# Taking the squares of the next batch out of the vector queue over four products

## The chip, the cores and the metric

The kernel runs on one core of one Trainium2 chip. The metric is the time of one execution on the device in microseconds (us). A profile records one execution; its span is some 1.8 us shorter than the time given for that execution, and the positions below (at 188.6 us, say) count from the span's start. PE is TensorE, DVE is VectorE, ACT is ScalarE; PEld is the loading of weights into PE. L735 and the like are lines of the kernel; behind the change, the lines from 637 on are higher by four (L735 became L739, L642 became L646).

## The reference

```python
scores = scale * q @ k.T                       # batch 8, 12 heads, 448 rows, 64 wide
attn   = np.maximum(scores, 0) ** 2 / 448
x      = (attn @ v)  -> (3584, 768)
h      = x @ w_in                              # 768 -> 2048
g      = np.maximum(h, 0) ** 2                 # relu, then the square
out    = g @ w_out                             # 2048 -> 768, float32
```

## The kernel before

All instructions are laid out by the program that writes the kernel: each engine then runs its own list, in order. Batches are handled in pairs. For each pair the kernel first computes h for its two batches and then `g @ w_out`, one *group* of two blocks of 128 rows after the other. A group is seven products of eight matmuls (a Strassen-Winograd scheme: seven products in place of eight, at the price of operand sums on DVE). Between them stand steps of the attention of later batches ("visits": scores on PE, relu on ACT, squares of `at` on DVE).

Relus and squares of g for the later batches of a pair are not put into DVE's list at once. They go into a queue, `due_g`, and are taken out where a rough model of time has room, or all at once when a group needs them:

```python
def put(d):                                     # take the first of a queue
    ready, cost, fn, _ = d.popleft()
    at_ve[0] = max(at_ve[0], at_pe[0], ready) + cost
    fn()
def fill(until):                                # as many as the model has room for
    for d in (due, due_g):                      # due: squares of the attention
        while d and max(at_ve[0], at_pe[0], d[0][0]) + d[0][1] <= until:
            put(d)
def flush_g(b):                                 # all that batch b and those before it have left
    while due_g and due_g[0][3] <= b:
        put(due_g)
...
def ahead(i, k=n):                              # operand sum s_i of group k
    if k < len(groups) and i not in sets[k]:
        flush_g(max(2 * p + (tb > 2) for p, tb in groups[k] if (p, tb) not in saved))
        sums(i, groups[k], sets[k])
...
def end6(): copy("u2"); ahead(3)                # after the third product: s3, read by the fifth
def end5(): ahead(4)                            # after the fourth: s4, read by the seventh
def end7(): copy("u3"); plus(1, c1, "u3")       # after the fifth: ACT copies u, DVE adds it (osb)
def end4(): ...; ahead(1, n + 1); ahead(2, n + 1)
...
def run():                                      # matmul f of product k of group n
    ...
    if f == 0 and k == 0:
        ahead(1); ahead(2)
    nc.tensor.matmul(acc[0][:, 0:HALF], lhsT=left()[:, f], rhs=right[:, f], ...)
    if f == KH - 1:
        end()
        fill(at_pe[0] + AFTER[k])
```

The first product of the next group is placed ahead of the sixth of the present one. It reads g directly, row block f with matmul f.

## Time and profile before

| | |
|---|---|
| time, median of the first 3 runs | 375.21 us (374.9 to 375.5) |
| span of the profiled run | 373.3 us |
| PE busy | 361.8 us, 97% |
| DVE busy | 279.7 us, 75% |
| ACT busy | 247.6 us, 66% |
| waits of PE, all | 6.0 us |

PE is the bound. The other engines matter where PE waits for them, and a wait on PE moves all that follows.

### The profile page before, as it was taken

The numbers are of one execution on the slowest core, as the hardware profiler recorded it, in microseconds if no ns is written. First come the engines' busy times: TensorE is split into PE (matmuls) and PEld (weight loads), VectorE is DVE, ScalarE is ACT, GpSimd is POOL, SyncE is SP. The second block draws the span as 40 slices with busy tenths as digits, with TensorE's granted clock in tenths as the row PEclk, the third lists the DMA queues.
The fourth block names the chain that finished last, engine by engine and source line by source line (L and its number), as shares of the span: only waits on it lengthen the run. The fifth ranks groups of instructions, "written<-read, shape, count | busy, mean of one in ns | idle before, by whom it ended". The sixth has DMA issues, their size and how long they took to land.

```text
span 373.3 us, 8793 instructions
## 1 busy us (share of the span) xinstructions
PE 361.8 (97%) x3600; PEld 230.7 (62%) x3600; DVE 279.7 (75%) x518; ACT 247.6 (66%) x370; POOL 107.1 (29%) x128
## 2 busy tenths in 40 slices
PE   7999999999999999999989999999999999999994
PEld 3554444445555777875545578887555689975663
DVE  1886677996766787798866758989966688995442
ACT  2997895796676999876546588887665885531220
POOL 8545431837442344431044044050000000000001
PEclk9999999999999999999999999999999999999999
DMA  7999999999999999997799699792233300002333
GB/s 115 199 204 205 205 204 158 122 149 132 215 171 137 171 103 100 114 107 62 136 143 108 151 175 83 92 100 52 49 87 87 84 2 2 2 0 68 95 91 87
DMA packets 121159, 42.64 MB, mean 114 GB/s; under 512 B 100832, under 2 KB 117760, under 8 KB 121120
## 3 DMA queue, kind: packets, MB, share of 16 engines
q0 software_dynamic: 82912, 23.01, 61.9%
q1 hardware_dynamic: 38048, 18.98, 25.7%
q8 instruction: 28, 0.46, 0.5%
q10 hardware_dynamic: 160, 0.10, 0.1%
q14 instruction: 11, 0.09, 0.1%
HBM read 45.61 MB, written 11.01 MB: 152 GB/s over the span
## 4 chain that ended last, share of the span: by engine, by line
PE 86%; DVE 5%; ACT 5%; issue 2%; DMA 1%; POOLq 0%; POOL 0%; DVEq 0%; ACTq 0%
PE mm L735 32%; PE mm L552 26%; PE slot L254 10%; PE mm L422 9%; PE slot L319 7%; ACT at L258 4%; DVE at L371 2%; DMA q<-in_q_dram 1%; PE slot L225 1%; DVE s L608 1%; DVE xt L285 1%; DVE osb L642 1%; DVE g L500 1%; PE mm L225 0%; ACT u L637 0%
## 5 line engine op out<-in xcount | busy, mean ns | idle before, releaser
L258 ACT ACTIVATE at<-slot 128x896 f16<-128x896 f32 x168 | 146.0, 920 | 28.0 <-PE slot L254 28.0
L371 DVE TENSOR_TENSOR at<-at 128x896 f16<-128x896 f16 x168 | 99.1, 618 | 11.4 <-ACT at L258 11.3
L108 POOL DMA_DIRECT2D qs<-in_q_dram x36 | 35.3, 983 | 116.9 <-DMA qT<-qs 109.8
L735 PEld LDWEIGHTS <-s 128*128 128x128 f16 x440 | 41.4, 98 | 33.2 <-issue 3.6
L254 PE MATMUL slot<-qT,kT 64*64 64x448 f16 x756 | 57.4, 360 | 1.6 <-ACT at L258 0.9
L552 PEld LDWEIGHTS <-w 128*128 128x128 f16 x576 | 54.3, 98 | 5.2 <-issue 4.3
L552 PE MATMUL mm<-xt,w 128*128 128x224 f16 x432 | 49.0, 259 | 0.0
L735 PEld LDWEIGHTS <-g 128*128 128x128 f16 x336 | 31.6, 98 | 26.2 <-issue 4.7
L552 PEld LDWEIGHTS <-ws 128*128 128x128 f16 x432 | 40.3, 98 | 4.7 <-issue 4.7
L735 PE MATMUL mm<-b,g 128*128 128x384 f16 x224 | 40.9, 326 | 1.9 <-DVE g L500 1.9
L735 PE MATMUL mm<-b,s 128*128 128x384 f16 x216 | 39.6, 327 | 0.3 <-DVE s L608 0.2
L422 PE MATMUL mm<-xt,w 128*128 128x448 f16 x192 | 39.8, 354 | 0.0
L642 DVE SCALAR_TENSOR_TENSOR osb<-mm,u 128x384 f32<-128x384 f32 (+1 forms) x30 | 16.2, 542 | 30.9 <-ACT u L637 19.8
L735 PE MATMUL mm<-t,s 128*128 128x384 f16 x224 | 39.3, 326 | 0.0
L108 POOL DMA_DIRECT2D ks<-in_k_dram x36 | 35.1, 976 | 10.2 <-DMA b<-in_moe_w_out_dram 5.8
L254 PEld LDWEIGHTS <-kT 64*64 64x64 f16 x756 | 19.6, 104 | 28.9 <-issue 23.9
L575 POOL DMA_DIRECT2D out_dram<-osb x2 | 1.1, 564 | 120.0 <-DVE osb L642 120.0
L637 ACT ACTIVATE u<-mm 128x384 f32<-128x384 f32 x28 | 13.8, 491 | 31.6 <-PE mm L735 30.4
L552 PE MATMUL mm<-x,ws 128*128 128x224 f16 x288 | 34.1, 259 | 0.0
L319 PE MATMUL slot<-at,vt 64*64 64x448 f16 x588 | 31.9, 350 | 0.2 <-DVE at L371 0.2
L500 DVE TENSOR_TENSOR g<-g 128x896 f16<-128x896 f16 x48 | 29.8, 620 | 1.1
L493 DVE TENSOR_TENSOR g<-mm,m 128x448 f16<-128x448 f32 x36 | 22.1, 620 | 10.4 <-PE mm L552 7.1
(69 smaller groups left out, 394.5 us busy)
## 6 DMA issues: line engine op xcount, KB each, us to landing
out_dram<-osb SPq DMA_DIRECT2D x52, 192.0 KB, 3.2
vt<-in_v_dram POOLq DMA_DIRECT2D x24, 224.0 KB, 6.1
qs<-in_q_dram POOLq DMA_DIRECT2D x36, 112.0 KB, 4.5
ks<-in_k_dram POOLq DMA_DIRECT2D x36, 112.0 KB, 5.2
w<-in_moe_w_in_dram POOLq DMA_DIRECT2D x8, 384.0 KB, 11.9
b<-in_moe_w_out_dram POOLq DMA_DIRECT2D x4, 768.0 KB, 17.1
q<-in_q_dram POOLq DMA_DIRECT2D x6, 224.0 KB, 7.7
k<-in_k_dram POOLq DMA_DIRECT2D x6, 224.0 KB, 8.1
```

Source lines behind the costliest of these rows:

```text
L108: nc.gpsimd.dma_start(out=t[:, :, hh, :], in_=heads(src, n)[:, hh].rearrange("p (j d) -> p j d", d=D))
L254: nc.tensor.matmul(ps[c, hh, 0:S], lhsT=kT[r, j, c], rhs=qT[r, :, c], start=True, stop=True)
L258: nc.scalar.activation(out=at, in_=ps[:, :, 0:S], func=AF.Relu, scale=SK)
L319: nc.tensor.matmul(ps[64 * hh:64 * hh + 64, hp, 0:S], lhsT=vt[r, hh, j * D:(j + 1) * D], rhs=at[r, hh, :], start=(j == 0), stop=(j == J - 1))
L371: lambda: nc.vector.tensor_mul(at, at, at), 0))
L422: nc.tensor.matmul(cell[0][:, 0:S], lhsT=w1[f // 4][:, m, (f % 4) * P:(f % 4 + 1) * P], rhs=xts[b][:, m, :], start=(m == 0), stop=(m == NM ...
L493: nc.vector.tensor_add(gs(s, hi, right), acc(s, y), keep[s, nm])
L500: due_g.append((t, 0.54, lambda: nc.vector.tensor_mul(g, g, g), b))
L552: nc.tensor.matmul(XY[s][y][:, r * Q:(r + 1) * Q], lhsT=left(k, i0 + 2 * s + r, m), rhs=right(k, m), start=(fresh and r == 0 and m == 0), ...
L637: nc.scalar.activation(out=t, in_=X[0][:, 0:HALF], func=AF.Copy, scale=CO)
L642: nc.vector.scalar_tensor_tensor(out=osb[row][:, c], in0=acc[0][:, 0:cc.stop - cc.start], scalar=CO, in1=keep[nm][:, cc], op0=ALU.mult, op ...
L735: nc.tensor.matmul(acc[0][:, 0:HALF], lhsT=left()[:, f], rhs=right[:, f], start=(fresh and f == 0), stop=(f == KH - 1), skip_group_check=n ...
```

## The change

The intent: put the squares that the next group will need into DVE's list evenly over the first four products of the present group, instead of leaving what the model found no room for to the moment at which the next group starts.

```diff
+            def needs(k):
+                return max(2 * p + (tb > 2) for p, tb in groups[k]
+                           if (p, tb) not in saved)
+
             def ahead(i, k=n):
                 if k < len(groups) and i not in sets[k]:
-                    flush_g(max(2 * p + (tb > 2) for p, tb in groups[k]
-                                if (p, tb) not in saved))
+                    flush_g(needs(k))
                     sums(i, groups[k], sets[k])
...
                     if f == KH - 1:
                         end()
+                        if k < 4 and n + 1 < len(groups):
+                            some = sum(d[3] <= needs(n + 1) for d in due_g)
+                            for _ in range(-(-some // (4 - k))):
+                                put(due_g)
                         fill(at_pe[0] + AFTER[k])
```

## The prediction

> **What bounds the kernel now.** I read the page first. TensorE (PE) is busy 361.8 of 373.3 us, VectorE (DVE) 279.7, ScalarE (ACT) 247.6, so the kernel ends when its matmul stream ends, and another engine costs time only where a matmul waits for it. So the second view is the list of waits for PE alone: what it waited for, us in total, times, longest. It has eight rows and 6.0 us in all; the three largest are
>
> ```profile
> PE mm L735 <- DVE g L500: 1.9, 1, 1.9
> PE slot L203 <- DVE zeros L157: 1.2, 1, 1.2
> PE slot L254 <- ACT at L258: 0.9, 4, 0.3
> ```
>
> The second row is the start-up. The first is a single wait of a product of the last matrix multiplication (L735) for a square of the batch (L500, the multiplication of g with itself), the very instruction that the change moves. Third view: the chain of waits, in order of time, around that place (start, length, what).
>
> ```profile
> 182.85 1.35 PE slot L319 x28
> 184.23 0.92 ACT xt L325
> 185.15 0.68 ACT at L258
> 185.83 0.04 issue
> 185.87 0.50 ACT u L637
> 186.39 0.56 DVE osb L642
> 186.95 1.07 DVE at L371 x2
> 188.02 0.55 DVE g L500
> 188.56 0.05 issue
> 188.61 0.50 PE mm L735 x2
> ```
>
> In nearly all the rest of this stretch the chain is PE from one line to the next. Here it leaves PE: two ACT evictions, an ACT copy u, the DVE sum that needs u, two attention squares, and only then the last square of g, which PE needs. Fourth view, the timeline of the same place, for the size of the loss:
>
> ```profile
> 185.61 1.14 PE L735 MATMUL mm<-b,g 128*128 128x384 f16 x6
> ...
> 188.61 0.11 PEld L735 LDWEIGHTS <-g 128*128 128x128 f16 x2 [2.25 <-DVE g L500]
> 188.61 0.50 PE L735 MATMUL mm<-b,g 128*128 128x384 f16 x2 [1.86 <-DVE g L500]
> ```
>
> Eight matmuls of a product take 1.30 us (one starts at 172.06, the next at 173.36), or 0.1625 each. Six started at 185.61, so the seventh was due at 185.61 + 6 x 0.1625 = 186.58. It started at 188.61: **2.03 us lost** (the view says 1.86, because it counts modelled ends; its row for weight loads says 2.25). The seventh and eighth row blocks of g are what the last square of the second batch of the pair writes.
>
> **What the Trainium skill says.** "TensorE: Matmul & The Clock Gate", section "Architectural detail: the array is 16× 32×32, not 1× 128×128", says that the queues of ACT and DVE are strictly first in, first out, and that only weight loads can be pulled ahead on PE. The trace agrees: the last square had its input at 185.33 (end of the relu L498 before it), yet stood behind the sum, which DVE idled 1.06 us for, until u came. "VectorE: DVE Perf Modes", section "The perf-mode tier table", gives a multiplication of two 16-bit tensors two elements per cycle and an operation on one tensor four. The trace agrees in order: 896 elements take 0.62 us squared and 0.38 us through the relu. The relus and squares keep these costs; only their places change. "TensorE: Matmul & The Clock Gate", section "Part 1: The HAM clock gate", says the clock is throttled after an idle window of about 3.4 us. A 2 us wait is shorter, and the table by stage has the granted clock at 1.00 from 164 to 290 us, so I expect no clock effect in either direction.
>
> **The change part by part.** The kernel builds its instruction order when it is written out: squares and relus of g sit in a queue, are taken out where a rough model of time has room, and all the rest at the last moment by the next product group. The change takes an even share of those that the next group needs out of the queue at the end of each of the first four products. Nothing is added or removed. Set beside each other, the two programs have the same order on PE, ACT, POOL and SP; on DVE 436 rows stay 436, and the order differs in two places only: one stretch of the second pair of batches (around 178 to 188 us) and one of the third (261 to 269 us). The first pair has no such squares in the queue, and in the last pair the order is the same.
>
> *Second pair, gain.* The new order from 177.55 is: square, relu (448), square, one attention square, two sums osb, relu, square, relu (896), three attention squares, the operand sum s3, square, relu, s4, the last square, and only now the sum that waits for u. Start-to-start times of DVE, from the timeline: square or attention square 0.53 to 0.54, relu 0.30 of either size with a square behind it where it shows, osb 0.47, s 0.60. Chained from 177.55 the two osb start at 179.45 and, held by PE as before, 180.0; the three attention squares at 181.6, 182.1, 182.7; s3 at 183.2 and ends at 183.9; the last square starts at 185.25 and ends at 185.9. The first product that reads s3 starts at 184.30, the attention product reads the last of its squares at about 183.6 (finished 182.8), and the seventh matmul is due at 186.58. So all three are met, by 0.35, 0.8 and 0.7 us: the whole 2.03 us go. Behind it the sums and attention squares come as they did, and DVE idles 2.6 us between 190 and 195, so nothing is handed on.
>
> *Third pair, loss.* Here PE waits for nothing from 252 to 285 us in the profile of before. The squares are pulled ahead of s3, which is on the path soon. The rows that matter, before:
>
> ```profile
> 260.99 0.27 DVE L498 TENSOR_SCALAR g<-g 128x448 f16<-128x448 f16 x1
> 261.50 0.56 DVE L642 SCALAR_TENSOR_TENSOR osb<-mm,m 128x384 f32<-128x384 f32 x1 [0.24 <-issue]
> 261.97 1.15 DVE L371 TENSOR_TENSOR at<-at 128x896 f16<-128x896 f16 x2
> 263.04 0.68 DVE L608 TENSOR_TENSOR s<-g 128x1024 f16<-128x1024 f16 x1
> ...
> 264.45 1.46 PE L735 MATMUL mm<-b,s 128*128 128x384 f16 x8
> ```
>
> s3 ends at 263.72, and the product that takes it as weights starts at 264.45: 0.73 us to spare. New order after the relu at 260.99: square, osb, relu, square, relu (896), two attention squares, s3. Chained: square 261.29, osb 261.83, relu 262.30, square 262.60, relu 263.14, attention squares 263.44 to 264.51, s3 264.51 to 265.19. At 336 us the profile has a product released by such an s3: it starts 0.06 after its end. So the product starts at 265.25 instead of 264.45: **0.80 us of new wait**. (Four instructions moved ahead, 0.54 + 0.30 + 0.54 + 0.30 = 1.68 us, less the 0.24 idle that they fill, is 1.44; 0.73 of it was slack; with 0.06 for the release that is 0.77, the same within the rounding of the pitches.) The next group's first product there did not wait in the kernel before, so the third pair gains nothing back. s4, wanted at 270.9, is ready near 267.7.
>
> Sum: 375.21 - 2.03 + 0.80 = **374.0 us**, 0.33% faster.
>
> **The rivals.** (1) *Gain alone*: s3 of the third pair is in time after all, because DVE gets through faster than my chain. For it: 0.7 us is only a little over one DVE instruction. Against: the order is fixed, each step is a measured pitch, and four instructions stand ahead. It would give 375.21 - 2.03 = 373.2. (2) *The wait moves*: in the second pair s3 or the attention squares come too late, and PE waits there for them. For it: they are delayed 1.7 us and s3 keeps only 0.35 us. If the margin were missed by half a microsecond, the time would be 374.5. If the entire gain were lost, 376.0. (3) *The gain is absorbed later*: PE comes 2 us earlier and meets a transfer or a backlog of DVE or ACT. For it: POOL waits for transposes and DVE is at 75%. Against: PE has no wait of over 0.4 us after 189 us, q and k are fetched two units ahead by the program, and the attention's steps shift with PE. It would give about 375. (4) *The end is not PE*: against it, the stream of matmuls runs unbroken from 339 us to the end, so a shift of it reaches the end whole.
>
> **Range and chances.** The three runs of before spread 0.6 us. Between gain alone (373.2) and a gain half lost (374.9) lies what I hold likely: 373.2 to 374.9, centre 374.0. Two per cent is 7.5 us; no wait in reach has that size, and the largest loss I can construct is below 2 us. Faster by 2%: 0.01, same 0.98, slower 0.01.
>
> **What would show each step.** Right: the list of PE waits no longer has the row for g L500 of 1.9 us; the chain around 186 us stays on PE; a new PE wait of about 0.8 us for DVE s L608 appears near 263 us (264.45 less the 2.03 gained), one row with one wait; PE's end 1.2 us earlier. Wrong: a wait for g L500 that remains at about 185 us, a wait for s L608 near 184 us, no wait near 263 us (then 373.2), or new waits for at L258 or a transposed tile after 190 us.

## The result, and the profile after

The change takes 373.82 us (median of 4 runs, 373.78 to 373.89), beside 375.36 us for the kernel before (median of 4 runs, three of them the runs above, and one of 376.62). The ratio is 0.9954, 95% interval 0.993 to 0.9978: 0.46% less time, which counts as the same at 2%. Ratios here are those of runs of the same rounds; they lie within 0.001 of the ratio of the mean times, so they are not the ratio of the medians.

First view after: the waits of PE, its two largest rows of nine.

```profile
PE slot L203 <- DVE zeros L157: 1.2, 1, 1.2
PE mm L739 <- DVE s L608: 0.9, 2, 0.7
```

The row for g L500, 1.9 us, is gone, and the row for s L608 has grown from 0.2 us in one wait to 0.9 in two. Second view: the chain of waits in the stretch that left PE for seven steps before (start, length, what).

```profile
182.73 1.32 PE slot L319 x28
184.05 0.19 PE slot L254 x4
184.24 2.71 PE mm L739 x16
186.94 0.50 PE slot L254 x8
187.45 4.01 PE mm L739 x24
```

It stays on PE. The eight matmuls of the next group's first product now run without a break, and DVE's timeline shows why: the last square is done at 185.73, ahead of the sum that waits for ACT's u.

```profile
185.12 0.61 DVE L500 TENSOR_TENSOR g<-g 128x896 f16<-128x896 f16 x1
186.26 0.56 DVE L646 SCALAR_TENSOR_TENSOR osb<-mm,u 128x384 f32<-128x384 f32 x1 [0.53 <-ACT u L641]
```

Third view: the timeline in the third pair.

```profile
261.35 1.15 DVE L371 TENSOR_TENSOR at<-at 128x896 f16<-128x896 f16 x2
262.42 0.68 DVE L608 TENSOR_TENSOR s<-g 128x1024 f16<-128x1024 f16 x1
...
260.98 1.47 PE L739 MATMUL mm<-t,s 128*128 128x384 f16 x8
263.16 1.47 PE L739 MATMUL mm<-b,s 128*128 128x384 f16 x8 [0.71 <-DVE s L608]
```

A product takes 1.31 us from start to start, so the second was due at 262.29 and started at 263.16: 0.87 us lost, for an operand sum s3 that ended at 263.10. The balance along PE's own landmarks:

| start on PE of | before | after | difference |
|---|---|---|---|
| second pair, product that reads s3 | 184.30 | 184.17 | -0.13 |
| second pair, scores behind the next group's first product | 189.04 | 186.88 | -2.16 |
| third pair, fourth product | 263.14 | 260.98 | -2.16 |
| third pair, scores behind the fifth product | 265.84 | 264.56 | -1.28 |
| the last product | 366.78 | 365.51 | -1.27 |

The 0.13 us lie ahead of both places, where the two programs are the same: it is a difference between two executions. Then 2.03 us are gained at once, 0.88 lost at once, and nothing else moves.

### The profile page after: what moved, and what is told of

Its sections match the earlier page's. It is cut to its first block, busy times and chain, and to the rows that moved or that the text cites. A ratio compares the mean times of both kernels' runs of the same rounds, so it can differ in the third digit from the quotient of the medians.

```text
span 372.0 us, 8794 instructions
## 1 busy us (share of the span) xinstructions
PE 361.2 (97%) x3600; PEld 230.4 (62%) x3600; DVE 278.6 (75%) x518; ACT 247.6 (67%) x370; POOL 107.6 (29%) x128
## 4 chain that ended last, share of the span: by engine, by line
PE 84%; DVE 7%; ACT 5%; issue 2%; DMA 1%; POOL 0%; POOLq 0%; DVEq 0%; ACTq 0%
PE mm L739 31%; PE mm L552 25%; PE mm L422 9%; PE slot L254 9%; PE slot L319 7%; ACT at L258 4%; DVE at L371 2%; DMA k<-in_k_dram 1%; DVE s L608 1%; DVE g L500 1%; PE slot L225 1%; DVE g L493 1%; DVE xt L285 1%; DVE osb L646 1%; DVE g L498 1%
## 5 line engine op out<-in xcount | busy, mean ns | idle before, releaser
L500 DVE TENSOR_TENSOR g<-g 128x896 f16<-128x896 f16 x48 | 29.8, 620 | 1.2
```

Of the source, the lines that this page charges most:

```text
L500: due_g.append((t, 0.54, lambda: nc.vector.tensor_mul(g, g, g), b))
```

## The experiments

Edits are given against the kernel with the change, unless said otherwise. All outputs were correct. The kernels of the first four experiments ran on one chip, those of the next four on another.

### 1. The second pair alone

```diff
-                        if k < 4 and n + 1 < len(groups):
+                        if k < 4 and n + 1 < len(groups) and rows[0][0] == 1:
```

> The puts of the change are made in the second pair of batches alone; the third pair keeps the order of the kernel before. Theory (the gain lies in the second pair, 2.03 us; the third pair only loses 0.87): 375.4 - 2.03 = 373.3, about 0.5 us under the full change; no PE wait for g L500 near 186 us and none for s L608 near 263 us. Rival (the two places are linked, the third pair waits because PE comes there 2 us earlier): the wait of 0.7 to 0.9 us near 263 us stays and the time is that of the full change, 373.8.

Measured: 372.99 us (372.78 to 373.21, 6 runs), ratio 0.9934. The list of PE waits has neither place; its last row is the one for s L608 that the kernel before has too (it lies in the last pair):

```profile
PE mm L739 <- DVE s L608: 0.2, 1, 0.2
```

Without the third pair's part the change is 0.8 us better (its own runs were taken in other rounds; the timelines give 0.87). The wait for s3 is not made by PE's coming there earlier: PE came as early here, and did not wait.

### 2. The third pair alone

```diff
-                        if k < 4 and n + 1 < len(groups):
+                        if k < 4 and n + 1 < len(groups) and rows[0][0] == 2:
```

> The puts are made in the third pair alone; the second pair keeps the order of before. Theory: the 1.9 us wait for g L500 stays, a new wait for s L608 of 0.7 to 0.9 us comes near 265 us, time 375.4 + 0.87 = 376.2. Rival (the third pair's order is harmless by itself and waits only when PE is early): no wait there and 375.4.

Measured: 376.00 us (375.83 to 377.5, 6 runs), ratio 1.0026. Both waits are there:

```profile
PE mm L739 <- DVE g L500: 1.9, 1, 1.9
...
PE mm L739 <- DVE s L608: 0.9, 2, 0.7
```

The two parts of the change are independent: the second pair's gains, the third pair's loses. The six runs fall into two groups, four of 375.83 to 376.00 and two of 377.42 and 377.5; this is taken up at experiment 9.

### 3. The spread begins behind s3

```diff
-                        if k < 4 and n + 1 < len(groups):
+                        if 2 <= k < 4 and n + 1 < len(groups):
```

`end()` of the third product puts s3 into DVE's list, and only then are squares taken out. Of DVE's 518 instructions, one square now stands ahead of one sum in the second pair, and one sum behind the squares in the third; the rest is the order of before.

> The same puts, but spread over the third and fourth products only, after the sum s3 is in DVE's queue. On DVE one square moves ahead of one osb sum in the second pair, and one osb sum moves behind the squares in the third; s3 keeps its place. Theory (a single square ahead of the sum that waits for u makes the whole gain, and the squares ahead of s3 the whole loss): both waits are gone, 375.4 - 2.03 = 373.3 or, if the third pair's loss is fully given back, 0.87 us under the full change, 372.95. Rival (the even spread over four products is what makes the gain): the wait for g L500 comes back, wholly or in part, 374 to 375.4.

Measured: 373.17 us (372.83 to 373.33, 6 runs), ratio 0.9937. Neither wait is there. The timeline of the second pair:

```profile
185.46 0.63 DVE L500 TENSOR_TENSOR g<-g 128x896 f16<-128x896 f16 x1
...
185.71 1.46 PE L739 MATMUL mm<-b,g 128*128 128x384 f16 x8
```

So the even spread is not what gains. One square, placed ahead of one sum, makes the whole of it; the rest of the spread only loses.

### 4. The square between the sum and the attention squares

Against the kernel before (in the second pair only):

```diff
                         end()
+                        if k == 4 and n + 1 < len(groups) and rows[0][0] == 1:
+                            flush_g(needs(n + 1))
                         fill(at_pe[0] + AFTER[k])
```

> The order of before with one change: in the second pair the last square stands between the osb sum that waits for u and the two attention squares, instead of behind all three. Theory: the sum still starts at about 186.4 when u is there, the square at 186.9, so PE goes on at 187.5 instead of 186.6; of the 2.03 us some 1.0 us stay and 1.07 are gained: 374.3. Rival (the loss is all due to the sum's wait for u): nothing is gained, 375.4. Rival (the loss is all due to the work ahead of it): 373.3.

Measured: 373.86 us (373.68 to 374.15, 6 runs), ratio 0.9957. The runs of before at 375 us in the same rounds have a median of 374.92 (7 of 11), so 1.06 us are gained. The profile:

```profile
186.27 0.56 DVE L646 SCALAR_TENSOR_TENSOR osb<-mm,u 128x384 f32<-128x384 f32 x1 [1.06 <-ACT u L641]
186.74 0.61 DVE L500 TENSOR_TENSOR g<-g 128x896 f16<-128x896 f16 x1
...
185.49 1.14 PE L739 MATMUL mm<-b,g 128*128 128x384 f16 x6
187.42 0.50 PE L739 MATMUL mm<-b,g 128*128 128x384 f16 x2 [0.79 <-DVE g L500]
```

The seventh matmul was due at 185.49 + 6 x 0.1625 = 186.47 and came 0.95 us later. The 2.03 us are thus made of two parts of about the same size: the two attention squares ahead of the square of g (1.08), and the sum with its wait for u (0.95). Neither rival holds.

### 5 and 6. How much may stand ahead of s3

Both put nothing at the end of the first and third product, one (5) or two (6) entries at the end of the second product in the third pair alone, and the rest at the end of the fourth.

```diff
-                            for _ in range(-(-some // (4 - k))):
+                            for _ in range(some if k == 3 else
+                                           min(some, 1) if k == 1 and rows[0][0] == 2 else 0):
```

(2 in place of 1 for experiment 6.)

> As the spread over the last two products, but in the third pair one square (0.54 us) is put ahead of s3. Theory (s3 has 0.73 us to spare in the kernel before, less 0.06 for the release and about 0.07 by which my chain was short): no wait for s3 or under 0.1 us; time that of the spread over the last two products. Rival (any square ahead of s3 costs its own length): 0.5 us more.

> As before it, but one square and one relu (0.74 to 0.84 us) ahead of s3. Theory: a wait for s3 of 0.1 to 0.25 us near 263 us, and the time longer by that than with the spread over the last two products. Rival (each costs its length): 0.8 us more.

Measured: 372.93 us (372.77 to 373.22) for one, 373.09 (372.86 to 373.5) for two, 6 runs each. With one square ahead of it, s3 ended at 262.31 and PE did not wait (the products start at 261.18 and 262.49, 1.31 apart). With a square and a relu:

```profile
261.61 0.68 DVE L608 TENSOR_TENSOR s<-g 128x1024 f16<-128x1024 f16 x1
...
260.99 1.47 PE L739 MATMUL mm<-t,s 128*128 128x384 f16 x8
262.35 1.48 PE L739 MATMUL mm<-b,s 128*128 128x384 f16 x8
```

1.36 in place of 1.31: a wait of 0.05 us, below the 0.1 to 0.25 that were expected, since the relu cost only 0.19 us with an attention square behind it (260.35 to 260.54), the least of what I had allowed for it. So 0.73 us of DVE work ahead of s3 costs 0.05. In the full change s3 starts another 0.82 us later, counted from the product before it (262.42 after 260.98, in place of 261.61 after 260.99), and PE loses another 0.82. The run times cannot tell 5 from 6; the timelines can.

### 7. All at the end of the first product

```diff
-                            for _ in range(-(-some // (4 - k))):
+                            for _ in range(some):
```

> All squares and relus that the next group needs are taken out of the queue at the end of the first product, none spread. Theory (what counts is what stands ahead of the operands that PE wants next): no wait for g L500; in the second pair the sum osb that frees the accumulator of the fourth product comes at 182.2 instead of 180.0, so PE waits some 1.7 us there; in the third pair s3 ends at 266.8 on the scale of before, PE loses 2.4 us in all. Time 375.4 - 2.03 + 1.7 + 2.4 = 377.4. Rival (earlier squares are always better, and the loss of the change has another cause): 373.8 or less.

Measured: 377.91 us (377.08 to 379.08, 6 runs), ratio 1.0058. Again two groups: 377.08 to 377.30 (three runs) and 378.52 to 379.08. The profile, of a run of 377.08:

```profile
181.97 0.55 DVE L646 SCALAR_TENSOR_TENSOR osb<-mm,m 128x384 f32<-128x384 f32 x1
...
182.57 1.46 PE L739 MATMUL mm<-t,s 128*128 128x384 f16 x8 [1.54 <-DVE osb L646]
...
264.81 1.46 PE L739 MATMUL mm<-t,s 128*128 128x384 f16 x8 [2.15 <-DVE osb L646]
266.49 1.47 PE L739 MATMUL mm<-b,s 128*128 128x384 f16 x8 [0.21 <-DVE s L608]
```

In the second pair the fourth product was due at 179.57 + 1.31 = 180.88: 1.69 us late. In the third it was due 0.50 us behind the scores that start at 262.09, at 262.59: 2.22 late, and its successor another 0.37. What held PE is the sum that empties an accumulator, behind the squares on DVE. Together -2.03 + 1.69 + 2.59 = +2.25 us on the 375.07 of before in these rounds (the median of its four runs near 375) would be 377.3, and the lower group is 377.1 to 377.3. "Earlier is better" is refuted: an instruction in DVE's list is late or early only by what PE wants from the list next.

### 8. The same in the last pair

Experiment 3, and in addition:

```diff
-                        fill(at_pe[0] + AFTER[k])
+                        if k > 1 or n > 0 or rows[0][0] < 3:
+                            fill(at_pe[0] + AFTER[k])
```

> The spread over the last two products, and in the last pair of batches no filling of DVE's queue behind the first two products of its first group, so that s3 stands ahead of one relu and two squares there too. PE waits 0.27 us for s3 at 336.9 us in the kernel before. Theory: this wait goes as well, 0.2 to 0.3 us under the spread over the last two products. Rival (that wait is made up for later): the same time.

Measured: 372.52 us (372.45 to 372.70, 6 runs), ratio 0.9909, the best of all, and 0.41 us below experiment 5, which ran on the same chip in the same rounds and has no wait in the second or third pair either. The kernel of experiment 5 has products at 331.98 (sixteen matmuls) and 334.93, so its s3 is 0.33 to 0.35 us late there (0.27 had been read before the run, from a view that counts modelled ends). Here they follow without a break:

```profile
331.78 2.76 PE L739 MATMUL mm<-t,s 128*128 128x384 f16 x16
334.38 1.46 PE L739 MATMUL mm<-b,s 128*128 128x384 f16 x8
```

### 9 to 12. Two groups of runs

The kernel before does not have one time. Of its runs some are near 375 and some near 376.6; so are those of experiments 2 and 7, which keep or make a wait of about 2 us. The kernels without such a wait (the change, experiments 1, 3, 4, 5, 6 and 8) have 40 runs, and none has a spread over 0.7 us. Experiment 9 meant to lengthen the wait; 10 to 12 are the kernel before, unchanged, for its profile.

Experiment 9, against the kernel before:

```diff
                     if f == 0 and k == 0:
+                        if rows[0] == (1, 3):
+                            for _ in range(6):
+                                nc.vector.tensor_mul(zeros, zeros, zeros)
                         ahead(1)
```

> The kernel before, with six extra squares of a small tile of zeros (448 elements each) ahead of the last square in the second pair, which makes the wait there some 1.9 us longer, near 3.9 us. The runs of before, and of the two kernels that keep or make waits near 2 us, fall into two groups 1.6 us apart (374.9 and 376.6); the kernels without such a wait do not. Theory (a wait of about 2 us lets the clock of TensorE be lowered for a while in those executions in which it falls badly): with 3.9 us the lower clock comes in nearly every execution, time 375.0 + 1.9 + 1.6 = 378.5, and the profile shows a stretch of clock below 1 behind the wait. Rival (the two groups have another cause): 376.9 and 378.5 in the same mixture, or the clock at 1.00 throughout.

> The kernel before, unchanged, for a profile of an execution of the slower group (376.6 us). Theory: if it is of that group, the granted clock falls behind 188.6 us for about 3.4 us, and the matmuls there are spaced twice as far. Rival: the clock is 1.00 there, and the 1.6 us lie at another place.

> As the look before it; again, since about half of the executions are of the slower group. The same is expected of it: a stretch of lower clock behind 188.6 us if it is a run near 376.6 us, none if it is near 375.

> As the two looks before it. The same is expected of it: a stretch of lower clock behind 188.6 us if it is a run near 376.6 us, none if it is near 375.

Experiment 9 missed its aim. The last square had already been taken out when the six stand-ins were put, so they landed behind it (2.52 us of them from 188.49), and the wait stayed 1.86 us by the view of waits. So it is `fill`, after the fifth product and with the attention squares first, that takes this square out in the kernel before, and not the `flush_g` of the next group. Time 375.31 us (374.94 to 376.58, 4 runs), ratio 0.9993. Beyond that it shows only that s1 and s2 of that group can come 2.4 us later for nothing.

The looks: 376.65, 374.95 and 375.22 us. The first is of the slower group. Its PE timeline, and the stretches with busy times, where PEclk (the granted clock) is the third number from the end:

```profile
188.37 0.50 PE L735 MATMUL mm<-b,g 128*128 128x384 f16 x2 [1.86 <-DVE g L500]
...
189.30 2.26 PE L735 MATMUL mm<-nt,g 128*128 128x384 f16 x8
191.36 2.40 PE L735 MATMUL mm<-b,s 128*128 128x384 f16 x8
193.59 1.46 PE L735 MATMUL mm<-b,g 128*128 128x384 f16 x8
...
189.30:192.70 3.40, 3.40 (x17) 1.69 (x14) 1.71 (x3) 2.25 (x4) 1.32 (x2) 0.58 1.65 115
192.70:193.60 0.90, 0.90 (x6) 0.44 (x5) 0.00 (x0) 0.00 (x0) 0.00 (x0) 0.69 1.21 197
193.60:200.00 6.40, 6.40 (x69) 3.32 (x67) 3.57 (x6) 3.08 (x5) 0.00 (x0) 1.00 0.86 195
```

The second, with the same wait, in the same place:

```profile
188.70:192.70 4.00, 4.00 (x30) 2.12 (x29) 2.87 (x5) 2.49 (x4) 2.11 (x3) 1.00 1.57 103
```

In the slower execution two products behind the wait take 2.06 and 2.23 us from start to start, in place of 1.31: 1.67 us, which is the distance of the two groups. The granted clock is at half for 3.4 us (0.42 x 3.40 + 0.31 x 0.90 = 1.7 us of lost clock, twice that at one half) and whole again by 193.6. The trace's clock record for the dip is 3.413 us long. So the wait cost 2.03 us in each of the four profiled executions of the kernel before, and a further 1.7 us in those where the clock dipped: 16 of the 36 runs that I have of it (1 of 4, 4 of 11, 7 of 11, 3 of 7 beside the kernels above, and 1 of 3 looks). Of all 88 runs whose granted clock is on record, the 21 of a slower group (15 of before, two of experiment 2, three of 7, one of 9) have a mean of 0.992 to 0.995, and the 67 others one of 0.996 to 1.000.

Why only in some: the 14 traces show a regularity, which no run was made to test. After the start of the kernel the clock is whole for 53 to 108 times 3.413 us before each fall, a whole number each time, so it changes on a fixed grid of windows of that length. In the slower look the window ahead of the dip runs from 186.43 to 189.84 and holds the whole wait; PE's records (with their modelled ends) cover 1.55 of its 3.41 us, 45%. The other profiles with this wait (before, experiments 2 and 9, the other looks) have no dip there. Their clock falls to half behind the last matmul, at 371.6 to 372.8, and 54 windows back from that lies a boundary at 187.3 to 188.5, within the wait; in the second look it cuts off only the last 0.06 us, and the window ahead of it is covered for 1.61 us, 47%. All 15 falls, 14 of them behind the last matmul, follow a window covered for 45% or less, and no window covered for 47% or more is followed by one. A wait of 1.9 us lies whole in a window of 3.41 in (3.41 - 1.9) / 3.41 = 44% of the cases, and 16 of 36 is 44%; so close an agreement is in part luck. No run moved the wait against the windows, and only one profile shows a dip behind a wait.

## Why the prediction was right or wrong

- **The bound and the place.** Right. PE's stream set the end, the wait for g L500 was the one the change removes, and the last product came 1.27 us earlier for a balance of 1.28.
- **Second pair, 2.03 us gained.** Right, to the hundredth in the landmarks. The chain of DVE starts, summed by hand, put the last square at 185.25 to 185.9; it ran from 185.12 to 185.73, in an execution that was 0.13 us early. s3, with the predicted 0.35 us of margin, was ended at 183.76 and wanted at 184.17: 0.41.
- **Third pair, 0.80 us lost.** Right in mechanism, 0.07 us small in size: 0.87. The prediction chained relu to square at 0.30; here one pair took 0.37 (258.83 to 259.20), and from that square on the chain came out as summed (3.90 us to the end of s3). The 0.30 was the shortest such pair and not the usual one: of the 145 in the 14 traces the middle one takes 0.37.
- **The sum, 374.0.** 373.82 measured; 0.13 of the 0.18 us between them lie ahead of both places. That the sum could start from 375.21 was luck: three runs of the faster group in a row come, at 16 slower ones in 36, in some (20/36)^3 = 17% of the cases. The rival of a gain alone (373.2) is refuted by the wait of 0.71 us, and is what experiments 1 and 3 do reach; the rival of a wait that moves within the second pair did not come; a gain absorbed later did not come. One end of the range doesn't follow from the working: with half of the 2.03 us lost it would be 375.21 - 1.01 + 0.80 = 375.0, not 374.9.
- **Two details of the working.** The square that matters in the second pair was not left to "the last moment by the next product group": `fill` took it out after the fifth product (experiment 9), which changes none of the sums. And the traces have 518 DVE instructions, not 436; in order they differ in the two places named and nowhere else.
- **The clock.** Wrong. "A 2 us wait is shorter, [...] so I expect no clock effect in either direction" took the clock from one profile, which happened to be of the faster group. The kernel before lost a further 1.7 us in 16 of 36 runs, and the change has none of it. Its mean gain is therefore larger than the 1.2 us of the sum: with a dip in one of the four runs of before in its own rounds it was 1.7 us (375.56 - 373.83).
- **What the change was for.** The even spread was the form, not the cause. Of its parts one square, moved ahead of a sum that waits for ACT, carries the gain (experiment 3), and what the spread moves ahead of s3 in the third pair takes 0.87 us back (experiments 1 and 2).

## What to carry to other kernels

On an engine that runs its list in order, ask of each instruction what the bounding engine wants from that list next, not whether it comes early: ahead of a sum that itself waits for a third engine, and of two attention squares, an urgent square is worth 2 us, ahead of an operand sum with 0.7 us to spare the same squares cost. Chain the start-to-start times of the new order by hand, against the times at which PE wants each result; it was good to a tenth of a microsecond here. And when a kernel's runs fall into two groups, take profiles until one is of the slower group.

## What the Trainium skill lacked or had wrong

- "TensorE: Matmul & The Clock Gate", section "Part 1: The HAM clock gate", has the clock fall after an idle window of about 3.4 us, and does not say how idle. Here it fell to half behind a wait of 1.9 to 2.0 us, in 16 of 36 runs going by their times and in one profile that shows it. Its length, 3.413 us, is that of the page's window, and one half is the page's factor. In the traces a window covered by PE's records for 45% was enough, and one covered for 47% was not. Waits of 0.9 us (the change, experiment 4) lowered it in none of 10 runs.
- The section "HAM oscillation — how this bites in real kernels" of the same page warns of gaps over some 3.4 us that come again and again. A single gap of 1.9 us was enough for 1.7 us more here.
- No page that I found gives what a DVE instruction loses when it reads the result of the one just ahead of it: from the start of a relu to that of the square that reads it there are 0.37 us for a relu of 448 elements (the middle of 145 pairs, 0.30 at least) and 0.42 for one of 896 (186 pairs), beside 0.18 to 0.19 and 0.30 at the least where the next instruction doesn't read it.
- None gives the time from the end of a DVE instruction to the start of the PE instruction that it releases: 0.05 to 0.06 us in this trace (188.56 to 188.61, 336.81 to 336.87, 263.10 to 263.16).
